# Attention, token mixer and channel mixer in one kernel: float64 weights unpacked without a sign pass, early hidden rows stored as float32, and a new order of all operations

## The chip, the cores and the metric

One core of one Trainium2 chip. The metric is the device time of one execution in microseconds; of several runs the median counts. Times inside an execution come from one profiled execution. Engines are named as in the profile: PE (matmul; PEld is its weight load), DVE (vector), ACT (scalar), POOL (GpSimd), SP (the queue that issues most DMAs).

## The reference, cut to what matters

```python
scores = np.matmul(q, k.T) / 8, masked above the diagonal     # 4 batches x 12 heads, 448 tokens, 64 wide
attn   = exp(scores - max) / (sum + 1e-9);  x = attn @ v      # x: 4 x 448 x 768
u  = x + (relu(x.T @ w_tok1) @ w_tok2).T                      # 448 -> 256 -> 448
y  = u + relu(u @ w_ch1) @ w_ch2                              # 768 -> 1536 -> 768
x_prev = y one token earlier (zeros first)
xk = mu_k*y + (1-mu_k)*x_prev;  xr = mu_r*y + (1-mu_r)*x_prev
out = sigmoid(xr @ w_r) * (relu(xk @ w_k)**2 @ w_v)           # 768 -> 1024 -> 768
```

The weights (w_tok1 to w_r) arrive as float64, q, k and v as float32. The output is float32.

## The kernel before, in words

The matmuls run on two-part numbers: each float32 operand is a rounded high part (ACT makes it by a copy) and the remainder, a low part (DVE subtracts). `mm3` issues three matmuls for each product: high x high, high x low, low x high.

A float64 weight is unpacked in halves of up to 384 columns by `split64` (weights of the token mixer, of w_ch1, w_ch2, w_r) or `load64` (w_k, w_v): SP loads the raw words into `raw`, ACT scales the upper words into `tmp` (`magnitude`), DVE clamps and shifts `tmp` (`shift`), merges the lower words (`assemble`), ACT writes the high part (`high`), DVE or POOL the low part (`low`). In stage 0 `magnitude` takes the absolute value, and a second pass of `assemble` (L307) puts the sign bit back. In stage 1 (`fold`) the sign travels through a Prelu with two slopes, and the second pass is not there.

Stage 0 (`schedule(0)`) holds, for each of the 24 pairs of heads: transposes of k and q (tiles `pt`, `kt`, `qt`), scores (`ps`), row maxima on DVE (`ms`, `nm`, L1396), exponentials on ACT (`e`, L1412), a reciprocal on DVE (`rc`, L1423 and L1426), the multiplication by it (`norm`, L1430, eight for each pair, on POOL or DVE), transposes of `e` on PE (`pe`, L1453), their copies (`et`, L238), the product with v (`pv`) and its transpose (`pn`). The six pairs of batch 0 are scored in float32 (L1375), the others in two parts (L1384). Every three pairs the token mixer follows (`ph`, `pu`, `tok_half`). `early_ch1` fills PE with part of the channel mixer: for batches 0 to 2 it computes 8 of the 12 blocks of relu(u @ w_ch1) (tile `pd`), makes their high and low parts (`relu_hi` L1696, `relu_lo` L1700, tile `he`), and stores both to DRAM (`h_d`). Its 144 groups of three matmuls are the only work in stage 0 that PE can do without a softmax in front of it, from the end of batch 0 on.

Stage 1 (`channel_mixing`, `schedule(1)`) runs batch 3, then 0, 1, 2 through the rest of the channel mixer (tiles `ph`, `acc`), then the gate (`pr`), the products with w_k (`pk`) and with w_v (`pv<-wv`). Where a block was computed early, `h_load` brings both parts back from `h_d` (tile `a`), after the ch2 step four back has begun (`seen[-4]`).

Every operation is registered by `op` with a due time, an engine (or two to choose from), a cost in us, and what it reads, writes and holds. `walk` plays the operations against each other: of those that could start next on an engine it takes the one with the lowest rank (the due time, shifted for some operations by `nudge` with the seeds `NUDGES`, in stage 0 alone), and where two engines are allowed, the one that ends sooner by the costs. The result is the program order of each engine, which the chip then follows; it also decides which `norm`, `low` and copies go to POOL, DVE or ACT.

Of the kernel before, what the change touches and what calls it, by code (L numbers as in the profile page):

```python
# [20 lines left out]
def kernel(  # L21
# [64 lines left out]
    h_d = dpool.tile([B - 1, 8, 128, 2, S], F32, name="h_d")  # L86
# [8 lines left out]
    LAT = {PE: 0.24, ACT: 0.2, DVE: 0.16, POOL: 0.12, SP: 2.6, NONE: 0.0}  # L95
# [3 lines left out]
    class Step:  # L99
        __slots__ = ("t", "eng", "cost", "f", "r", "w", "u", "mode", "phase", "left", "pre", "next", "alt")  # L100
# [4 lines left out]
    state = {"phase": 0, "mode": "F", "dma": 0.0}  # L105

    def op(t, eng, cost, f, *args, r=(), w=(), u=(), mode="F", alt=None):
        x = Step()
        x.t, x.eng, x.cost, x.mode, x.phase = t, eng, cost, mode, state["phase"]
        x.f, x.alt = (f, args), {eng: cost, **(alt or {})}  # L110
        x.r, x.w, x.u = list(r), list(w), list(u)
        steps.append(x)
        for k in x.w:
            makers.setdefault(k, []).append(x)
        for k in x.u:
            users.setdefault(k, []).append(x)

    def walk(mine, rank):
# [35 lines left out]
        while len(out) < len(mine):  # L154
# [31 lines left out]
            free[eng] = s + cost  # L186
            end = s + cost + LAT[eng]
# [18 lines left out]
    NUDGES = tuple(1000000 + n for n in (  # L206
# [5 lines left out]
    ))  # L212
# [31 lines left out]
    LO_BITS = float(np.uint32(896 + 128 << 20).view(np.float32))  # L244
    HI_BITS = float(np.uint32((1151 + 128 << 20) - 1).view(np.float32))
# [6 lines left out]
    def split64(t, key, use, dest, src, pp, n, blocks=False, lead=0):  # L252
# [5 lines left out]
        box, fold = {}, state["phase"] == 1  # L258
# [9 lines left out]
        def magnitude():  # L268
            tmp = wraw.tile([128, 384], F32, tag="tmp", name="tmp")
            box["tmp"] = tmp[:pp, :n]  # L270
            if fold:
                nc.scalar.activation(
                    box["tmp"], box["raw"][:, :, 1].bitcast(F32), AF.Prelu, scale=TINY, alpha=FOLD
                )
                return
            nc.scalar.activation(
                box["tmp"], box["raw"][:, :, 1].bitcast(F32), AF.Abs, scale=65536.0
            )

        def shift():  # L280
            tmp = box["tmp"]
            bits = tmp.bitcast(I32)
            if fold:
                nc.vector.tensor_scalar(
                    out=tmp, in0=tmp, scalar1=NEG_BITS, scalar2=POS_BITS, op0=ALU.max, op1=ALU.min
                )
                nc.vector.tensor_scalar(
                    out=bits, in0=bits, scalar1=3, scalar2=None, op0=ALU.logical_shift_left
                )
                return  # L290
            nc.vector.tensor_scalar(
                out=tmp, in0=tmp, scalar1=LO_BITS, scalar2=HI_BITS, op0=ALU.max, op1=ALU.min
            )
            nc.vector.tensor_scalar(
                out=bits, in0=bits, scalar1=4, scalar2=1,
                op0=ALU.logical_shift_left, op1=ALU.logical_shift_right,
            )

        def assemble():
            raw = box["raw"]  # L300
            bits = box["tmp"].bitcast(I32)
            nc.vector.scalar_tensor_tensor(
                bits, raw[:, :, 0], 29, bits, op0=ALU.logical_shift_right, op1=ALU.bitwise_or
            )
            if fold:
                return
            nc.vector.scalar_tensor_tensor(  # L307
# [1480 lines left out]
```

## Time and profile before

| what | value |
|---|---|
| median of 3 runs | 917.48 us (917.46 to 920.13) |
| the profiled execution's own time | 917.56 us |
| its span, first to last instruction | 915.8 us |
| mean granted TensorE clock | 0.997 |
| PE busy | 899.3 us (98%) |
| DVE, ACT, POOL busy | 650.3, 500.8, 76.0 us |

The span is what the trace covers; the 1.8 us between it and the time of the same execution lie around it. A matmul's record is longer than the time until the next can start, so a busy PE in these views may still have lost some of its time. Stage 0 ends, as far as PE shows it, at about 354 us.

### The profile page before, as it was taken

To read this page: it belongs to the slowest core of one execution; us is meant where nothing else is said; L and a number is where in the kernel's file an instruction comes from. 1 tells how busy PE (TensorE), PEld (TensorE's weight loads), DVE (VectorE), ACT (ScalarE), POOL (GpSimd) and SP (SyncE) were. 2 spreads that over 40 slices of the span, in tenths; PEclk is the share of its full clock that TensorE was granted. 3 is DMA by queue.
4 is the path that set the end of the run, shared out by engine and by line. 5 is a ranking of instruction groups with operands and counts; after the bars stand their busy time and mean duration, and the time that the engine had idled before them with its cause. 6 is when DMAs were issued, how large, how long until landed. Compare 5 with 4: busy or idle time off the path is not lost.

```text
span 915.8 us, 15743 instructions
## 1 busy us (share of the span) xinstructions
PE 899.3 (98%) x5340; PEld 804.4 (88%) x5340; DVE 650.3 (71%) x1547; ACT 500.8 (55%) x1186; POOL 76.0 (8%) x169
## 2 busy tenths in 40 slices
PE   7899999999999999999999999999999999999997
PEld 4577887888888889999999999999999999999997
DVE  6999899985576655777774646559644676789873
ACT  6987777775566654445442324236634566763330
POOL 3332122210110010000000000000000000000000
PEclk9999999999999999999999999999999999999999
DMA  9644666463444212558595895867874264576552
GB/s 199 152 138 105 176 198 175 121 199 99 110 124 130 73 65 83 163 155 296 168 330 207 281 331 201 275 221 239 275 227 138 97 219 128 174 260 185 177 151 61
DMA packets 174128, 162.66 MB, mean 178 GB/s; under 512 B 87584, under 2 KB 160800, under 8 KB 174048
## 3 DMA queue, kind: packets, MB, share of 16 engines
q1 hardware_dynamic: 173120, 161.43, 57.6%
q8 instruction: 42, 0.69, 0.3%
q10 hardware_dynamic: 928, 0.23, 0.1%
q14 instruction: 38, 0.31, 0.1%
HBM read 108.66 MB, written 51.38 MB: 175 GB/s over the span
## 4 chain that ended last, share of the span: by engine, by line
PE 95%; ACT 1%; DVE 1%; POOL 1%; DMA 0%; issue 0%; SPq 0%; POOLq 0%; ACTq 0%
PE acc L554 6%; PE acc L552 6%; PE acc L553 6%; PE pe L1453 5%; PE pv L1469 5%; PE ph L552 4%; PE ph L553 4%; PE ph L554 4%; PE ps L1384 4%; PE pk L552 4%; PE pk L554 4%; PE pk L553 4%; PE pv L553 4%; PE pv L554 4%; PE pv L552 4%; PE pd L552 3%
## 5 line engine op out<-in xcount | busy, mean ns | idle before, releaser
L1412 ACT ACTIVATE e<-ms,nm 112x448 f32<-112x448 f32 (+3 forms) x192 | 100.6, 532 | 17.1 <-DVE nm L1396 16.3
L553 PE MATMUL acc<-a,w 128*128 128x448 f32 x288 | 105.2, 365 | 0.0
L552 PE MATMUL acc<-a,w 128*128 128x448 f32 x288 | 105.2, 365 | 0.0
L554 PE MATMUL acc<-a,w 128*128 128x448 f32 x288 | 105.2, 365 | 0.0
L1396 DVE CUSTOM_DVE_ANT_0 ms<-ps,mask 112x448 f32<-112x448 f32 (+3 forms) x192 | 77.8, 442 | 18.7 <-PE ps L1384 12.2
L238 ACT COPY et<-pe 112x448 f32<-112x448 f32 x109 | 53.5, 539 | 35.5 <-PE pe L1453 35.3
L1430 POOL TENSOR_SCALAR e<-e,rc 112x224 f32<-112x224 f32 (+3 forms) x94 | 52.6, 576 | 211.3 <-DVE rc L1426 133.2
L1453 PE MATMUL pe<-ident,e 112*112 112x112 f32 x480 | 61.8, 267 | 4.9 <-POOL e L1430 2.5
L552 PE MATMUL pv<-wv,kk 128*128 128x384 f32 x196 | 65.5, 334 | 0.0
L554 PE MATMUL pv<-wv,kk 128*128 128x384 f32 x196 | 65.5, 334 | 0.0
L553 PE MATMUL pv<-wv,kk 128*128 128x384 f32 x196 | 65.5, 334 | 0.0
L1453 PEld LDWEIGHTS pe<-ident,e 112*112 112x112 f32 x480 | 50.9, 136 | 14.6 <-POOL e L1430 5.3
L553 PE MATMUL pk<-a,wk 128*128 128x448 f32 x168 | 61.9, 368 | 0.0
L554 PE MATMUL pk<-a,wk 128*128 128x448 f32 x168 | 61.8, 368 | 0.0
L552 PE MATMUL pk<-a,wk 128*128 128x448 f32 x168 | 61.8, 368 | 0.0
L552 PE MATMUL pd<-a,w 128*128 128x448 f32 x144 | 58.1, 403 | 0.0
L552 PEld LDWEIGHTS acc<-a,w 128*128 128x128 f32 x288 | 54.1, 188 | 4.3
L553 PEld LDWEIGHTS acc<-a,w 128*128 128x128 f32 x288 | 54.1, 188 | 4.2
L554 PEld LDWEIGHTS acc<-a,w 128*128 128x128 f32 x288 | 54.1, 188 | 4.2
L418 ACT CAST kk<-a 128x512 fp32r<-128x512 f32 x49 | 30.2, 621 | 49.6 <-PE pv L554 36.5
L554 PE MATMUL pr<-w,a 128*128 128x384 f32 x168 | 56.1, 334 | 0.0
L553 PE MATMUL pr<-w,a 128*128 128x384 f32 x168 | 56.1, 334 | 0.0
(142 smaller groups left out, 2243.2 us busy)
## 6 DMA issues: line engine op xcount, KB each, us to landing
raw<-in_moe_w_ch_dram SPq DMA_DIRECT2D x48, 384.0 KB, 3.7
h_d<-he SPq DMA_DIRECT2D x24, 448.0 KB, 2.9
a<-h_d SPq DMA_DIRECT2D x24, 448.0 KB, 5.4
x_d<-t SPq DMA_DIRECT2D x48, 224.0 KB, 3.5
a<-x_d SPq DMA_DIRECT2D x48, 224.0 KB, 4.4
a<-u_d SPq DMA_DIRECT2D x36, 224.0 KB, 4.1
raw<-in_moe_w_v_dram SPq DMA_DIRECT2D x16, 384.0 KB, 5.5
raw<-in_moe_w_k_dram SPq DMA_DIRECT2D x16, 384.0 KB, 4.1
```

What stands on the lines that cost most here:

```text
L238: nc.scalar.copy(o, i) if by == ACT else nc.vector.tensor_copy(o, i)
L418: nc.scalar.copy(dest()[0], src())
L552: nc.tensor.matmul(o, lh, rh, start=start and i == 0, stop=False, skip_group_check=skip)
L553: nc.tensor.matmul(o, lh, rl, start=False, stop=False, skip_group_check=skip)
L554: nc.tensor.matmul(o, ll, rh, start=False, stop=stop and i == n - 1, skip_group_check=skip)
L1384: nc.tensor.matmul(T["s", j, c], T["q"][r, x, qc], T["k"][r, y, :n], start=i == 0, stop=i == 2,)
L1396: nc.vector.tensor_tensor_reduce(out=ms[:, :n], in0=T["s", j, c], in1=mask[:, S - n:], scale=-0.125, scalar=BIG, op0=ALU.add, op1=ALU.min, ...
L1412: nc.scalar.activation(T["e", j][:, eoff[c]:eoff[c + 1]], T["ms", j, c][:, :n], AF.Exp, bias=T["nm"][:, j, c:c + 1], scale=-1.0, accum_out ...
L1430: (nc.gpsimd if by == POOL else nc.vector).tensor_scalar(out=ec, in0=ec, scalar1=T["rc"][:, j, c:c + 1], scalar2=1.0, op0=ALU.mult, op1=AL ...
L1453: nc.tensor.transpose(pe[:CP, o + (c - kc) * CP:o + (c - kc + 1) * CP], T["e", j][:, eoff[c] + kc * CP:eoff[c] + (kc + 1) * CP], ident[:CP ...
L1469: nc.tensor.matmul(T["pv"][64 * j:64 * j + 64, kc * CP:S], T["vn"][:, kc, j, :], T["et"][:, o:o + S - kc * CP], start=kc == 0, stop=kc == 2,)
```

## The change

1. `split64` always uses the Prelu form: the sign pass of stage 0 (28 instructions on DVE, L307) is gone. `shift` is split into two operations, `clamp` and `shift`, in `split64` and `load64`, so that other operations may come between them.
2. `early_ch1` no longer makes two parts: one Relu on ACT writes float32 rows (4 buffers in place of 2), and `h_d` holds half the bytes. In stage 1 each of the 24 blocks is loaded as float32 and then rounded on ACT (`h_hi`) and subtracted on DVE (`h_lo`).
3. The planner: other costs, an own delay between operations of one engine that depend on each other (`SELF`), and a resource `port` that operations marked `sb` hold one at a time; other due times (`PAIR`, `EV`, the early weights); other seeds. All engines get a new order.

```diff
-    h_d = dpool.tile([B - 1, 8, 128, 2, S], F32, name="h_d")
+    h_d = dpool.tile([B - 1, 8, 128, S], F32, name="h_d")
...
+    SELF = {PE: 0.0, ACT: 0.12, DVE: 0.11, POOL: 0.1, SP: 0.0, NONE: 0.0}
...
-                s = max(s, here if e == eng != SP else end)
+                s = max(s, here + SELF[e] if e == eng != SP else end)
+            if x.sb:
+                s = max(s, state["port"])
...
-    NUDGES = tuple(1000000 + n for n in (
+    NUDGES = (
...
             nc.scalar.activation(
-                box["tmp"], box["raw"][:, :, 1].bitcast(F32), AF.Abs, scale=65536.0
+                box["tmp"], box["raw"][:, :, 1].bitcast(F32), AF.Prelu, scale=TINY, alpha=FOLD
+            )
...
-            if fold:
-                return
-            nc.vector.scalar_tensor_tensor(
-                bits, raw[:, :, 1], -(2 ** 31), bits, op0=ALU.bitwise_and, op1=ALU.bitwise_or
...
-        op(t, DVE, 0.1 + (0.66 + slow) * g, shift, r=[("mag", k)], w=[("bit", k)], u=u[1:])
+        op(t, DVE, 0.09 + 0.19 * g, clamp, r=[("mag", k)], w=[("clp", k)], u=u[1:], sb=True)
+        op(t, DVE, 0.09 + 0.19 * g, shift, r=[("clp", k)], w=[("bit", k)], u=u[1:], sb=True)
...
-        nc.sync.dma_start(h3s[b, j].bitcast(F32), h_d[b, j])
+        nc.sync.dma_start(raw(h3s[b, j]), h_d[b, j])
+
+    def h_hi(b, j):
+        part_hi(h3s[b, j])
+
+    def h_lo(b, j):
+        part_lo(h3s[b, j])
...
+                op(t - 2.2 * BEAT, ACT, 0.46, h_hi, b, j, r=[("hr", b, j)], w=[("hhi", b, j)], u=[a2])
+                op(t - 2.2 * BEAT, DVE, 0.54, h_lo, b, j, r=[("hhi", b, j)], w=[("hh", b, j)], u=[a2], sb=True)
...
-    PAIR = (11.0, 13.0, 15.0, 16.0)
+    PAIR = (10.0, 13.5, 14.5, 14.5)
...
                     op(
-                        s0 + 9.1 + 2 * j + 0.1 * i, POOL, (0.43, 0.53, 0.6, 0.7)[c], norm, j, c,
-                        r=[("rc", g)], w=[("no", j, c, g)], u=[("e", j, g), ("st", g)],
-                        alt={DVE: (0.24, 0.31, 0.42, 0.55)[c]},
+                        s0 + 9.1 + 2 * j + 0.1 * i, POOL, (0.34, 0.43, 0.52, 0.615)[c], norm, j, c,
+                        r=[("rc", g)], w=[("no", j, c, g)], u=[("e", j, g), ("st", g)], sb=True,
+                        alt={DVE: (0.19, 0.245, 0.31, 0.37)[c]},
...
-            def relu_lo(j):
-                t = G["h", j]
-                nc.vector.scalar_tensor_tensor(
-                    t[:, 1], G["p", j][:, :S], 0.0, t[:, 0].bitcast(F32), op0=ALU.max, op1=ALU.subtract
-                )
...
-            ch_weight(n, 60 + 14.0 * n, 7, f"w{n}")
+            ch_weight(n, 70 + 16.0 * n, 8, f"w{n}")
```

What the planner makes of it, counted over the built programs: of the 192 `norm` multiplications 98 stood on DVE and 94 on POOL, now 134 and 58. Of the 28 `low` passes of the early weights 18 stood on POOL, now 10. Of the 120 copies of `pe` to `et` 11 stood on DVE, now 16, the rest on ACT. PE does the same matmuls; it changes 108 times between whole-array matmuls and those that use half of the rows (`ps`) or of the columns (`pv<-et`), now 102 times.

Three places in the order follow. First, the start of the program on DVE, before (tmp and raw are a float64 half of a token-mixer weight on its way, ms and nm the row maxima of pair 0):

```order
L291 TENSOR_SCALAR tmp<-tmp 112x256
L294 TENSOR_SCALAR tmp<-tmp 112x256
L302 SCALAR_TENSOR_TENSOR tmp<-raw,tmp 112x256
L307 SCALAR_TENSOR_TENSOR tmp<-raw,tmp 112x256
L1396 ISA ms,nm<-ps,mask 112x448
```

and now (w_127 is the token-mixer weight, its low part written here):

```order
L282 TENSOR_SCALAR tmp<-tmp 112x256
L289 TENSOR_SCALAR tmp<-tmp 112x256
L295 SCALAR_TENSOR_TENSOR tmp<-raw,tmp 112x256
L282 TENSOR_SCALAR tmp<-tmp 112x256
L289 TENSOR_SCALAR tmp<-tmp 112x256
L295 SCALAR_TENSOR_TENSOR tmp<-raw,tmp 112x256
L304 TENSOR_TENSOR w_127<-tmp,w_127 112x256
L1394 ISA ms,nm<-ps,mask 112x112
```

Two halves and a low part now stand ahead of the first row maximum, where one half stood.

Second, POOL in pairs 0 and 1 (e is the exponentials, rc the reciprocal; the rows behind the second pass on w_127 are those of pair 1), before:

```order
L316 TENSOR_TENSOR w_127<-tmp,w_127 112x256 x2
L1430 TENSOR_SCALAR e<-e,rc 112x112
L1430 TENSOR_SCALAR e<-e,rc 112x448 x2
L1430 TENSOR_SCALAR e<-e,rc 112x224
L1430 TENSOR_SCALAR e<-e,rc 112x112
L1430 TENSOR_SCALAR e<-e,rc 112x336
```

and now:

```order
L304 TENSOR_TENSOR w_127<-tmp,w_127 112x256
L1428 TENSOR_SCALAR e<-e,rc 112x112 x2
L1428 TENSOR_SCALAR e<-e,rc 112x336
L1428 TENSOR_SCALAR e<-e,rc 112x224
L1428 TENSOR_SCALAR e<-e,rc 112x448 x3
```

One weight pass instead of two stands in front of the multiplications of pair 1. In both orders POOL has six of that pair's eight (the last of the three 448-wide ones now belongs to pair 2, which has six on POOL too, where it had four).

Third, DVE in stage 1 while batch 0 goes through the mixer, now, with buffer numbers (a_5843 is an early block that came back from DRAM, ph a block of this stage, w and tmp a weight of the gate):

```order
L295 SCALAR_TENSOR_TENSOR tmp_5882<-raw_5816,tmp_5882 128x384
L627 SCALAR_TENSOR_TENSOR a_5904<-ph_5867,a_5904 128x448
L304 TENSOR_TENSOR w_5911<-tmp_5882,w_5911 128x384
L599 TENSOR_TENSOR a_5843<-a_5843 128x448
L282 TENSOR_SCALAR tmp_5931<-tmp_5931 128x384
```

and at the like place before:

```order
L410 TENSOR_TENSOR tmp_5874<-tmp_5969,tmp_5874 128x384
L637 SCALAR_TENSOR_TENSOR a_5988<-ph_5955,a_5988 128x448
L284 TENSOR_SCALAR tmp_5997<-tmp_5997 128x384
L287 TENSOR_SCALAR tmp_5997<-tmp_5997 128x384
L302 SCALAR_TENSOR_TENSOR tmp_5997<-raw_5939,tmp_5997 128x384
```

The subtraction for the early block is new on DVE; it stands behind a subtraction that needs PE (`a_5904<-ph_5867`), and between the end of that block on PE and the first matmul on a_5843 PE has 73 other matmuls to do. Over the 24 early blocks this distance is 55 to 181 matmuls.

## Rows read from the trace of the kernel before

**Rows 1.** The page: busy time of the engines; chain that ended last.
```profile
PE 899.3 (98%) x5340; PEld 804.4 (88%) x5340; DVE 650.3 (71%) x1547; ACT 500.8 (55%) x1186; POOL 76.0 (8%) x169
...
PE 95%; ACT 1%; DVE 1%; POOL 1%; DMA 0%; issue 0%; SPq 0%; POOLq 0%; ACTq 0%
```

**Rows 2.** Windows by stage: busy us and (x instructions), PEclk, DMA share, GB/s.
```profile
0.00:100.00 100.00, 88.56 (x625) 64.09 (x627) 85.05 (x275) 79.11 (x234) 30.00 (x55) 0.98 0.63 150
100.00:355.00 255.00, 254.96 (x1830) 213.60 (x1827) 187.32 (x543) 171.17 (x472) 41.01 (x73) 1.00 0.45 130
355.00:617.00 262.00, 262.00 (x1295) 242.92 (x1294) 170.28 (x357) 101.72 (x196) 4.25 (x36) 1.00 0.70 234
...
809.00:916.00 107.00, 101.78 (x588) 101.46 (x586) 78.82 (x135) 31.77 (x55) 0.00 (x0) 0.99 0.51 153
```

**Rows 3.** Waits of PE: total us, times, longest.
```profile
PE pt L1350 <- DMA kn<-in_k_dram: 4.1, 1, 4.1
PE pe L1453 <- POOL e L1430: 2.5, 4, 1.7
PE ps L1375 <- ACT qt L1354: 1.3, 2, 0.7
PE pe L1453 <- DVE e L1430: 1.1, 1, 1.1
```

**Rows 4.** Windows of 2 us around the fall of the clock.
```profile
28.00:30.00 2.00, 1.24 (x9) 1.24 (x10) 1.97 (x6) 0.53 (x1) 1.89 (x4) 0.78 0.12 47
30.00:32.00 2.00, 2.00 (x13) 1.89 (x11) 1.90 (x7) 1.95 (x6) 0.41 (x1) 0.50 0.01 2
32.00:34.00 2.00, 2.00 (x16) 1.39 (x16) 1.93 (x6) 2.00 (x6) 0.25 (x1) 0.86 0.69 195
```

**Rows 5.** Timeline of PE: start us, us, what [idle before].
```profile
27.40 0.31 PE L1453 MATMUL pe<-ident,e 112*112 112x112 f32 x1 [1.71 <-POOL e L1430]
28.76 3.49 PE L1453 MATMUL pe<-ident,e 112*112 112x112 f32 x19 [1.05 <-DVE e L1430]
...
40.27 2.43 PE L1453 MATMUL pe<-ident,e 112*112 112x112 f32 x20 [0.57 <-DVE xh L1496]
```

**Rows 6.** Timeline of PE in stage 1, two matmuls in a row.
```profile
503.60 0.36 PE L553 MATMUL ph<-a,w 128*128 128x448 f32 x1
503.80 0.36 PE L554 MATMUL ph<-a,w 128*128 128x448 f32 x1
```

**Rows 7.** Groups of DVE by form, 0 to 355 us: busy us, mean ns.
```profile
L1700 DVE SCALAR_TENSOR_TENSOR he<-pd,he 128x448 fp32r<-128x448 f32 x24 | 14.9, 620 | 15.6 <-ACT he L1696 15.3
...
L1430 DVE TENSOR_SCALAR e<-e,rc 112x448 f32<-112x448 f32 x21 | 12.7, 603 | 0.4
...
L307 DVE SCALAR_TENSOR_TENSOR tmp<-raw,tmp 128x384 int32<-128x384 int32 x20 | 11.2, 558 | 0.7
...
L1430 DVE TENSOR_SCALAR e<-e,rc 112x112 f32<-112x112 f32 x24 | 9.7, 406 | 0.5
```

**Rows 8.** Timeline of DVE: one multiplication by itself.
```profile
322.49 0.45 DVE L1430 TENSOR_SCALAR e<-e,rc 112x448 f32<-112x448 f32 x1
```

**Rows 9.** Groups of POOL by form, 0 to 355 us.
```profile
L1430 POOL TENSOR_SCALAR e<-e,rc 112x448 f32<-112x448 f32 x27 | 19.0, 705 | 59.1 <-DVE rc L1426 32.9 <-ACT xh L1492 18.3 <-ACT h L1600 7.9
...
L316 POOL TENSOR_TENSOR w<-tmp,w 128x384 fp32r<-128x384 f32 x12 | 12.5, 1040 | 29.8 <-ACT w L312 25.0 <-PE pt L1350 4.7
```

**Rows 10.** Timeline: the first row maximum on DVE.
```profile
8.97 0.62 DVE L1396 CUSTOM_DVE_ANT_0 ms<-ps,mask 112x448 f32<-112x448 f32 x1 [0.90 <-PE ps L1375]
```

**Rows 11.** Groups of DVE and ACT by form, 355 to 916 us.
```profile
L609 DVE TENSOR_TENSOR a<-a 128x448 fp32r<-128x448 f32 x42 | 24.4, 619 | 3.7 <-ACT a L606 3.6
...
L606 ACT CAST a<-a 128x448 fp32r<-128x448 f32 x42 | 22.6, 566 | 5.7 <-DMA a<-x_d 3.3 <-DMA a<-u_d 2.1
```

**Rows 12.** The page: DMA issues, KB each, us to landing.
```profile
a<-h_d SPq DMA_DIRECT2D x24, 448.0 KB, 5.4
...
a<-x_d SPq DMA_DIRECT2D x48, 224.0 KB, 4.4
```

More of the change, by code (lines that the diff above doesn't have):

```diff
@@ L94 @@
     PE, ACT, DVE, POOL, SP, NONE = "PE", "ACT", "DVE", "POOL", "SP", "-"
-    LAT = {PE: 0.24, ACT: 0.2, DVE: 0.16, POOL: 0.12, SP: 2.6, NONE: 0.0}
+    LAT = {PE: 0.24, ACT: 0.2, DVE: 0.16, POOL: 0.15, SP: 2.6, NONE: 0.0}
+    SELF = {PE: 0.0, ACT: 0.12, DVE: 0.11, POOL: 0.1, SP: 0.0, NONE: 0.0}
     MODE, STICK, WAIT = 0.1, 1.5, 0.08
@@ L99 @@
     class Step:
-        __slots__ = ("t", "eng", "cost", "f", "r", "w", "u", "mode", "phase", "left", "pre", "next", "alt")
+        __slots__ = ("t", "eng", "cost", "f", "r", "w", "u", "mode", "phase", "left", "pre", "next", "alt", "sb")
     steps, makers, users = [], {}, {}
@@ L104, with op @@
     free = {e: 0.0 for e in (PE, ACT, DVE, POOL, SP, NONE)}
-    state = {"phase": 0, "mode": "F", "dma": 0.0}
-    def op(t, eng, cost, f, *args, r=(), w=(), u=(), mode="F", alt=None):
+    state = {"phase": 0, "mode": "F", "dma": 0.0, "port": 0.0}
+    def op(t, eng, cost, f, *args, r=(), w=(), u=(), mode="F", alt=None, sb=False):
         x = Step()
+        x.sb = sb
         x.t, x.eng, x.cost, x.mode, x.phase = t, eng, cost, mode, state["phase"]
@@ L186, in walk @@
             free[eng] = s + cost
+            if x.sb:
+                state["port"] = s + cost
             end = s + cost + LAT[eng]
@@ L252, in split64 @@
     def split64(t, key, use, dest, src, pp, n, blocks=False, lead=0):
[L258 removed]
+        box = {}
         def load():
@@ L397, in load64 @@
         op(
-            t, ACT, 0.18 + 0.37 * g, magnitude, r=[("raw", k)] + ([last[1]] if last else []),
+            t, ACT, 0.04 + 0.41 * g, magnitude, r=[("raw", k)] + ([last[1]] if last else []),
             w=[("mag", k)], u=u,
         )
-        op(t, DVE, 0.1 + 0.66 * g, shift, r=[("mag", k)], w=[("bit", k)], u=u[1:])
-        op(t, DVE, 0.05 + 0.5 * g, assemble, r=[("bit", k)], w=[key], u=u)
+        op(t, DVE, 0.09 + 0.19 * g, clamp, r=[("mag", k)], w=[("clp", k)], u=u[1:], sb=True)
+        op(t, DVE, 0.09 + 0.19 * g, shift, r=[("clp", k)], w=[("bit", k)], u=u[1:], sb=True)
+        op(t, DVE, 0.05 + 0.43 * g, assemble, r=[("bit", k)], w=[key], u=u, sb=True)
         return (lambda: box["tmp"]), u[1]
@@ L410, in f @@
             (eng.tensor_add if plus else eng.tensor_sub)(o(), x(), y())
-        op(t, DVE, 0.06 + 0.5 * g, f, r=r, w=[key], u=use)
+        op(t, DVE, 0.05 + 0.42 * g, f, r=r, w=[key], u=use, sb=True)
     def split32(t, key, r, use, dest, src, g=1.0):
@@ L422, in low @@
             (nc.gpsimd if by == POOL else nc.vector).tensor_sub(lo, src(), hi.bitcast(F32))
-        op(t, ACT, 0.18 + 0.33 * g, high, r=r, w=[key + ("hi",)], u=use)
+        op(t, ACT, 0.04 + 0.37 * g, high, r=r, w=[key + ("hi",)], u=use)
         op(
-            t, DVE, 0.06 + 0.5 * g, low, r=[key + ("hi",)], w=[key], u=use,
+            t, DVE, 0.05 + 0.42 * g, low, r=[key + ("hi",)], w=[key], u=use, sb=True,
         )
@@ L1119, in total @@
                     def total(name, o, where, x, r, u):
-                        op(te, DVE, 0.63, k_sum, n, q, o, where, x, r=end + [(r, n, q)], w=[(name, n, q)], u=u)
+                        op(te, DVE, 0.54, k_sum, n, q, o, where, x, r=end + [(r, n, q)], w=[(name, n, q)], u=u)
                     if f == "11":
-                        op(te, ACT, 0.54, k_copy, n, q, r=end, w=[("kvx", n, q)], u=[kb["a"], zx])
+                        op(te, ACT, 0.44, k_copy, n, q, r=end, w=[("kvx", n, q)], u=[kb["a"], zx])
                     elif f == "s2":
@@ L1126, in channel_mixing @@
                     elif f == "12":
-                        op(te, ACT, 0.54, k_relu, n, q, r=end, w=[("kr", n, q)], u=[kb["a"], zr])
+                        op(te, ACT, 0.44, k_relu, n, q, r=end, w=[("kr", n, q)], u=[kb["a"], zr])
                     elif f == "s3":
```

144 lines of the change are left out of this document (62 added, 82 removed), and 11 rows, old and new, of the table NUDGES.

## The prediction

> **What bounds the kernel now.** I read the page first. PE is busy for 899.3 of 915.8 us, and PE makes up 95% of the chain that ended last [rows 1]: whatever the change takes off DVE, ACT, POOL or the DMA queues counts only where PE waits for it. The windows by stage show where that can be [rows 2]. From 100 to 355 us PE is busy for 254.96 of 255 us, from 355 to 617 us for 262 of 262; only the first 100 us (88.56 busy) and the end (809 to 916 us, 101.78 busy) have holes. The end is the last evacuation and store behind the last matmul, which the change leaves alone. So 11.4 us of idle PE in the first 100 us are what there is to win, less what can't go away: 4.1 us before the first k has landed [rows 3]. That leaves 7.3 us.
>
> Two things stand behind this idle time and are lost with it. A matmul's record (0.36 us) is longer than the time to the next start (0.20 us) [rows 6], so each wait hides some 0.16 us inside a busy record; for the seven waits of rows 3 behind the first, that is 1.1 us. And the clock: behind the pause that ends with POOL's and DVE's multiplications of pair 1 (1.71 and 1.05 us idle [rows 5]) the granted clock is 0.78, 0.50 and 0.86 in three windows of 2 us [rows 4], so it stood at the lower of its two levels, 1.2 GHz, for a stretch; the missing shares are (0.22 + 0.50 + 0.14) x 2 = 1.7 us. In rows 5 it can be seen: 19 transposes take 3.49 us there, 20 of them 2.43 us at 40.27. The pot in the early part is thus 7.3 + 1.1 + 1.7 = 10.1 us.
>
> **The change part by part.** I sum against the profiled execution's own time, 917.56 us (915.8 of span and 1.8 around it); the median of the runs, 917.48, is the same within 0.1 us.
>
> *Sign pass.* 20 instructions of 0.558 us [rows 7] and 8 narrower ones go: 11.2 to 15.6 us of DVE, I take 14. *Second part of the early blocks.* 24 x 0.620 = 14.9 us of DVE go [rows 7]. Both leave DVE, which is not the bound; they lie beside PE work.
>
> *What the new order puts on DVE in return.* 36 multiplications, between 0.406 us (112 wide) and 0.603 us (448 wide) as they run now [rows 7], about 18 us; 5 copies of et, 448 wide and from PSUM as L1700 is, so some 0.62 us each, 3 us; 8 low parts at no more than the 0.558 of a like pass, up to 4.5 us. That is 25.5 us back for 29 us removed: DVE ends 3.5 us lighter, not 29. It may be more: a 448-wide multiplication that ran by itself took 0.45 us [rows 8], against the mean of 0.603. With 94 such operations on POOL now and 58 after, more of the 134 on DVE run by themselves; at 0.15 us each this is up to 20 us. POOL loses 36 multiplications (at most 0.705 us each) and 8 low parts (at most 1.04 us) [rows 9], up to 33.7 of its 76 us.
>
> The Trainium skill bears on that ("SBUF — State Buffer", section "Who interferes with whom"): a DVE operation of this kind and a GpSimd operation hold a shared port pair in turn, and the later one blocks for the whole instruction of the other. The trace agrees in kind, with 0.45 against a mean of 0.603 us. Taken literally it speaks against the move: if each moved multiplication had to sit out one 448-wide one on POOL, the 36 would cost up to 36 x (0.45 + 0.705) = 41.6 us of DVE, and DVE would end 20 us heavier. By the mean row it ends lighter.
>
> *What PE gets of it, term by term.* (a) The waits for the multiplications, 2.5 + 1.1 = 3.6 us [rows 3], with five of the hidden tails (0.8) and the clock (1.7): 6.1 us. The order speaks for a part only: pairs 3 and on have most multiplications on DVE, but pairs 1 and 2 have six of eight on POOL, behind one weight pass rather than two, and their last one on DVE stands behind row maxima of the next pair. I take half, -3.0; the bounds are 0 and -6.1. (b) The other idle time in the first 100 us, 7.3 - 3.6 = 3.7 us: 1.3 of it waits for ACT's copies of qt [rows 3], which the change doesn't touch, the rest is spread over single waits for copies and parts, which meet shorter queues where the early weights are unpacked later (from 70 in place of 60, every 16 in place of 14). I take a third, -1.2; bounds 0 and -3.7. (c) At the start DVE now has three passes of a second weight half and a low part ahead of the first row maximum, at most 4 x 0.558 = 2.2 us. DVE stood idle for 0.90 us just there, waiting for the scores [rows 10]; what is left, up to 1.3 us, delays pair 0, while PE goes on with the transposes of pairs 1 and 2. I take +0.3. (d) Six changes of the array's mode fewer: taken as 0, at most one hidden tail each, -1.0. (e) From 100 to 355 us: 0, PE has no idle time to give there, and this is what hides the removed passes.
>
> *Early blocks through DRAM as float32.* New in stage 1: 24 x (0.566 + 0.619) us on ACT and DVE [rows 11], 13.6 and 14.9 us, in the stretch from 355 to 617 us. Their cover: ACT is busy for 101.7 and DVE for 170.3 of 262 us there [rows 2], and each load is released four ch2 steps ahead of its use, 4 x 18 matmuls x 0.20 = 14.4 us. Of these the load takes some 4.4 us (the 224 KB rows of x_d, against 5.4 for the present 448 KB [rows 12]), the two passes 1.2 us: 8.8 us stay for standing in the queues of ACT and DVE. The order gives 55 to 181 matmuls, at least 11 us, between the nearest work of PE that the new subtraction stands behind and its use. I take 0; if the cover is gone, what is late is the ch2 step itself, and behind it all of PE. Halved traffic brings nothing either, since no matmul of this stage waits now.
>
> Sum: 917.6 - 3.0 - 1.2 + 0.3 = 913.7 us.
>
> **The rivals.** *More than the pot.* The views of idle time may understate the early loss: PE retires 625 matmuls in the first 100 us and 1830 in the 255 behind them [rows 2], 6.25 against 7.18 per us. If the first 100 us ran at the later rate, they would take 87 us, and the kernel 904.5 us. For it: DVE (85) and ACT (79) are both near full there, so PE is led by the softmax of pairs 0 to 7, and DVE gets relief. Against it: the mix of shapes differs, the 4.1 us at the start stay, and ACT's work hardly shrinks.
>
> *No change.* The multiplications that PE waited for on POOL are waited for on DVE, behind row maxima; pair 1 still pauses, the clock still falls, and (c) eats the rest: 917.6 - 1.2 + 0.3 or so, 916.7 us. For it: two of the first three pairs keep six on POOL.
>
> *Slower, by the new rounding passes.* ch2 needs an early block, whose subtraction stands on DVE behind weight halves and behind a subtraction that waits for PE. It decides once the two queues hold a block for more than the 8.8 us left over; each block that is then late by 0.3 us costs 0.3 us of PE, 24 of them 7.2 us: 924.8 us, or 921 with the gain of the early part. For it: on blocks with a distance of 73 matmuls up to eleven instructions, of 0.56 to 0.62 us at most, stand in between on DVE, some 6 us of the 8.8, and raw loads share SP's queue. Against it: today's loads of twice the size end no wait of PE.
>
> The clock could widen the middle case in either direction: a new pause like that of rows 5 costs its length and 1.7 us. The Trainium skill tells the same of a kernel that idles and falls back to the low clock ("TensorE: Matmul & The Clock Gate", section "HAM oscillation — how this bites in real kernels"); rows 4 are this kernel's instance.
>
> **How the numbers follow.** What three runs of this kernel can tell from no change is about 0.3%, 2.8 us. Gain of part of the pot, 910 to 914.7 us: 0.36, the likeliest, its own range 910 to 914.7. Gain at or beyond the pot, 902 to 910: 0.20. Within 0.3% (914.7 to 920.3): 0.26. Slower by the rounding passes or by new early pauses: 0.18. That makes faster 0.56, same 0.26, slower 0.18. The range leaves out the best few hundredths below 904 and about one in eight above 921.5, where the rounding passes would cost more than the early part brings.
>
> **What would show it.** Right: in the first 100 us PE's idle time falls from 11.4 to some 7 us, the wait of pe for e on POOL shrinks below 1.5 us, the end of stage 0 comes 3 to 5 us sooner than 354 us, and from there on every stage is as long as before, with no wait of acc for a tile a. DVE's mean for a multiplication falls from 0.603 (448 wide) towards 0.45 us. Wrong: idle PE between 355 and 617 us; a low clock at a new place; stage 0 sooner by more than 10 us, which would say that the lost time lay inside busy records; or a stage 0 of the old length.

## The result, and the profile after

| | before | after |
|---|---|---|
| median | 917.48 us (917.46 to 920.13, 4 runs) | 906.59 us (906.09 to 907.14, 4 runs) |
| span of the profiled execution | 915.8 us | 904.1 us |
| mean granted clock | 0.997 | 1.000 |

The ratio is 0.9874, interval 0.9856 to 0.9893: 10.9 us faster, where 3.8 us were forecast. The time is inside the range, near its lower end. The two profiled executions lie 11.5 us apart (917.56 and 906.09); the traces below are theirs.

The page of the kernel after, busy time of the engines:

```profile
PE 892.8 (99%) x5340; PEld 802.9 (89%) x5340; DVE 628.4 (70%) x1568; ACT 507.7 (56%) x1205; POOL 47.8 (5%) x125
```

PE does as many matmuls as before in 6.5 us less of recorded time [rows 1]: part of what was saved had been counted as busy. The windows by stage, after (columns as in [rows 2]):

```profile
0.00:100.00 100.00, 93.62 (x692) 68.79 (x693) 86.97 (x308) 87.67 (x260) 22.84 (x43) 1.00 0.70 167
100.00:355.00 255.00, 255.00 (x1819) 218.13 (x1817) 163.36 (x523) 163.52 (x450) 19.92 (x41) 1.00 0.37 105
355.00:617.00 262.00, 262.00 (x1304) 243.67 (x1304) 188.56 (x397) 120.67 (x235) 4.56 (x36) 1.00 0.69 220
```

The same cut where PE's stages end, before and then after (stage 0; stage 1 up to the first `pr`):

```profile
0.00:354.44 354.44, 342.96 (x2449) 277.16 (x2450) 271.87 (x816) 250.08 (x704) 71.01 (x128) 1.00 0.50 135
354.44:617.09 262.65, 262.65 (x1297) 243.53 (x1296) 170.87 (x358) 102.02 (x198) 4.25 (x36) 1.00 0.70 234
...
0.00:342.86 342.86, 336.48 (x2448) 275.66 (x2449) 243.08 (x814) 245.88 (x698) 42.76 (x84) 1.00 0.47 124
342.86:605.52 262.66, 262.66 (x1298) 243.45 (x1296) 184.90 (x391) 117.12 (x230) 4.56 (x36) 1.00 0.67 216
```

In the first 100 us PE starts 692 matmuls and not 625, its idle time falls from 11.44 to 6.38 us, and DVE is as full as before (86.97 against 85.05): the passes that went made room for others. The waits of PE, over the whole kernel after:

```profile
PE pt L1348 <- DMA kn<-in_k_dram: 4.0, 1, 4.0
PE ps L1373 <- ACT qt L1352: 0.9, 2, 0.7
PE pe L1451 <- ACT qt L1352: 0.5, 1, 0.5
PE ps L1373 <- ACT kt L1352: 0.3, 1, 0.3
PE pe L1451 <- DVE et L246: 0.3, 1, 0.3
PE ps L1373 <- DVE nm L1394: 0.2, 1, 0.2
```

Both waits for `e` of [rows 3], 3.6 us, are gone. With them went the fall of the clock: where [rows 4] have 0.78, 0.50 and 0.86, the same windows after read

```profile
28.00:30.00 2.00, 2.00 (x15) 1.53 (x17) 2.00 (x8) 2.00 (x8) 0.00 (x0) 1.00 0.46 141
30.00:32.00 2.00, 2.00 (x16) 1.11 (x14) 1.97 (x11) 2.00 (x8) 0.13 (x1) 1.00 0.90 277
32.00:34.00 2.00, 1.98 (x19) 1.14 (x16) 2.00 (x13) 2.00 (x8) 2.00 (x4) 1.00 0.17 52
```

How far the kernel after leads on PE. Since the order differs, the first four marks are points at which PE has issued the same matmuls in both kernels, counted by kind from the timelines (us from the span's start):

| mark | before | after | lead |
|---|---|---|---|
| 56 matmuls, before the transposes of `e` of pair 0 | 17.25 | 16.42 | 0.8 |
| 176 matmuls, behind those of pair 1 | 37.56 | 32.68 | 4.9 |
| 605 matmuls, 9 of them for early blocks | 97.44 | 89.13 | 8.3 |
| 1356 matmuls | 199.35 | 188.93 | 10.4 |
| first `ph` of stage 1, 2448 matmuls | 354.44 | 342.86 | 11.6 |
| first `pr` (stage 1's mixer done) | 617.09 | 605.52 | 11.6 |
| end of the span | 915.77 | 904.14 | 11.6 |

All of it is won in stage 0: 4.1 us around pair 1, 3.4 more up to the third mark, and 3.3 behind it. Stage 1 takes 262.65 us from `ph` to `pr` before and 262.66 after.

**What happens at pair 1.** PE after, as a timeline:

```profile
21.64 2.11 PE L1467 MATMUL pv<-et,vn 112*64 112x448 f32 x16
23.67 0.64 PE L1373 MATMUL ps<-kt,qt 64*112 64x224 f32 x4
24.24 0.60 PE L1348 MATMUL pt<-ident,qn 112*128 112x112 f32 x4
24.70 0.62 PE L1485 MATMUL pn<-ident,xT 128*112 128x128 f32 x4
25.16 0.55 PE L1348 MATMUL pt<-ident,kn 112*128 112x112 f32 x4
25.63 1.01 PE L1373 MATMUL ps<-kt,qt 64*112 64x448 f32 x4
26.57 2.44 PE L1451 MATMUL pe<-ident,e 112*112 112x112 f32 x20
```

The 20 transposes of pair 1 start without a wait and take 2.44 us, as the later pair of [rows 5] did. The reciprocal that releases their multiplications, on DVE, before and then after, and the six multiplications on POOL after:

```profile
26.24 0.17 DVE L1423 TENSOR_SCALAR rc<-sm 112x8 f32<-112x8 f32 x1
```
```profile
22.98 0.17 DVE L1421 TENSOR_SCALAR rc<-sm 112x8 f32<-112x8 f32 x1
...
23.49 3.01 POOL L1428 TENSOR_SCALAR e<-e,rc 112x112 f32<-112x112 f32 x6 [0.98 <-DVE rc L1424]
```

POOL is no faster and has as many of them. They run 3.3 us sooner, beside five steps of PE for pairs 0, 2, 3 and 4 that stand in front of the transposes; before, PE came to the transposes at 25.70 us with nothing else in front of them, and the reciprocal had not been started.

### The profile page after: what moved, and what is told of

Its sections match the earlier page's. It is cut to its first block, busy times and chain, and to the rows that moved or that the text cites. A ratio compares the mean times of both kernels' runs of the same rounds, so it can differ in the third digit from the quotient of the medians.

```text
span 904.1 us, 15752 instructions
## 1 busy us (share of the span) xinstructions
PE 892.8 (99%) x5340; PEld 802.9 (89%) x5340; DVE 628.4 (70%) x1568; ACT 507.7 (56%) x1205; POOL 47.8 (5%) x125
## 4 chain that ended last, share of the span: by engine, by line
PE 94%; ACT 3%; DVE 1%; DMA 1%; issue 0%; SPq 0%
PE acc L544 6%; PE acc L542 6%; PE acc L543 6%; PE pv L1467 5%; PE pe L1451 4%; PE ph L542 4%; PE ph L544 4%; PE ph L543 4%; PE pk L544 4%; PE pk L543 4%; PE pk L542 4%; PE pv L544 4%; PE pv L543 4%; PE pv L542 4%; PE ps L1382 3%; PE pd L542 3%
## 5 line engine op out<-in xcount | busy, mean ns | idle before, releaser
L1410 ACT ACTIVATE e<-ms,nm 112x336 f32<-112x336 f32 (+3 forms) x192 | 100.5, 530 | 12.5 <-DVE nm L1394 11.7
L599 DVE TENSOR_TENSOR a<-a 128x448 fp32r<-128x448 f32 x84 | 51.0, 627 | 19.1 <-ACT a L596 19.0
L246 ACT COPY et<-pe 112x448 f32<-112x448 f32 x104 | 50.9, 540 | 21.5 <-PE pe L1451 21.4
L596 ACT CAST a<-a 128x448 fp32r<-128x448 f32 x84 | 46.0, 567 | 24.7 <-DMA a<-h_d 20.2
L1451 PE MATMUL pe<-ident,e 112*112 112x112 f32 x480 | 57.6, 261 | 0.9 <-ACT qt L1352 0.5
L543 PE MATMUL pr<-w,a 128*128 128x384 f32 x168 | 56.1, 334 | 0.0
```

Of the source, the lines that this page charges most:

```text
L246: nc.scalar.copy(o, i) if by == ACT else nc.vector.tensor_copy(o, i)
L543: nc.tensor.matmul(o, lh, rl, start=False, stop=False, skip_group_check=skip)
L596: nc.scalar.copy(t[:, 0], raw(t))
L599: nc.vector.tensor_sub(t[:, 1], raw(t), t[:, 0].bitcast(F32))
L1410: nc.scalar.activation(T["e", j][:, eoff[c]:eoff[c + 1]], T["ms", j, c][:, :n], AF.Exp, bias=T["nm"][:, j, c:c + 1], scale=-1.0, accum_out ...
L1451: nc.tensor.transpose(pe[:CP, o + (c - kc) * CP:o + (c - kc + 1) * CP], T["e", j][:, eoff[c] + kc * CP:eoff[c] + (kc + 1) * CP], ident[:CP ...
```

## The experiments

Three questions: does the lighter work or the order bring the gain, do the places of the multiplications matter, and what in the order does it. The kernel before, run beside them, took 917.5 to 918.0 us (medians); ratios are to it.

### Lighter work and order, one without the other

`new_heavy`: the order of the kernel after with the 28 sign passes and the 24 passes over the early blocks put back, each right behind the pass that feeds it; the second kind writes a tile that nothing reads.

```diff
+            if first:
+                nc.vector.scalar_tensor_tensor(
+                    bits, box["raw"][:, :, 1], -(2 ** 31), bits, op0=ALU.bitwise_and, op1=ALU.bitwise_or
...
+                t = ud.tile([128, S], F32, tag="hx", name="hx", bufs=2)
+                nc.vector.scalar_tensor_tensor(t, G["p", j][:, :S], 0.0, G["h", j], op0=ALU.max, op1=ALU.subtract)
```

> The changed kernel in its own order, with the removed DVE passes put back: the 28 sign passes, and 24 passes that read pd behind the Relu and write an unused tile. If the lighter DVE brought the gain, most of the 10.9 us is lost again, 914 to 918 us. If the new order brought it, the passes go beside PE work and the time stays within 3 us of 906.6.

922.34 us, ratio 1.0052 (1.0037 to 1.0067). `old_light`: the order of the kernel before without both kinds of passes; the early blocks lack their low part (the high part stands in DRAM twice, so that loads and bytes stay).

```diff
-            nc.vector.scalar_tensor_tensor(
-                bits, raw[:, :, 1], -(2 ** 31), bits, op0=ALU.bitwise_and, op1=ALU.bitwise_or
-            )
...
-                nc.sync.dma_start(h_d[b, j], G["h", j].bitcast(F32))
+                nc.sync.dma_start(h_d[b, j], G["h", j].bitcast(F32).unsqueeze(1).to_broadcast([128, 2, S]))
```

> The kernel before in its own order, without the 28 sign passes (Prelu in place of Abs) and without the 24 passes for the low part of the early blocks; both halves of a row in DRAM hold the high part, so the low part of these blocks is left out. If the lighter DVE brought the gain, 906 to 910 us. If the order did, 915 to 918 us.

916.52 us, ratio 0.9987 (0.9978 to 0.9997). So the four corners are 917.5 (old order, old work), 916.5 (old, light), 922.3 (new, old work) and 906.6 (new, light): lighter work alone gives about 1 us, the new order alone costs 5, together they give 11. `new_heavy` is slower than either of its two theories allowed. (Each order was planned for its own work and tuned by its own list of nudges, so the corners show how an order fits its work, and not what an order is worth by itself; `new_heavy` also keeps the new rounding passes of stage 1.) In the old order the relief doesn't reach PE: it still waits 2.0 us for POOL's and 1.8 for DVE's multiplications. In the new order with the old work PE is starved far beyond the early part; windows of `new_heavy` (PE busy first):

```profile
100.00:150.00 50.00, 46.75 (x332) 38.35 (x331) 48.23 (x141) 37.78 (x100) 3.69 (x5) 1.00 0.60 168
150.00:200.00 50.00, 47.70 (x349) 39.41 (x349) 35.52 (x111) 32.96 (x93) 5.71 (x10) 1.00 0.48 132
```

Next, which of the two reliefs, each put back alone in the new order (`new_sign`, `new_low`: one of the two pieces of the diff above).

> The changed kernel with its order, and the 28 sign passes alone put back on DVE (20 of them some 0.56 us), not the 24 passes over the early blocks. Both together cost 15.8 us. Theory of DVE's load (what counts is how much DVE has to do in stage 0): the sign passes are half of the added time, so 913 to 916. Theory of the one bank (the passes over the early blocks cost nearly all, since pd has a single bank that comes free only behind its second reader): 907 to 909.5. Theory of the first pairs (it is the weights unpacked in the first 60 us that hold up the softmax): 917 or more, with a wait of pe for e and a granted clock below 1 between 20 and 40 us.

> The changed kernel with its order, and only the 24 DVE passes that read pd behind ACT's Relu put back (their result goes into a tile that nothing reads). DVE's load: 913 to 916. One bank: 918 to 922, with waits of pd for DVE's hx and the first pd where the changed kernel has it (63.6 us). First pairs: 909 to 911, since these passes stand behind 64 us.

913.87 us (0.9957, 0.9944 to 0.9971) and 912.71 us (0.9942, 0.9930 to 0.9954): 7.3 us for 28 passes (14.9 us of DVE in `new_sign`: 20 of 0.559, 4 of 0.528 and 4 of 0.392), 6.1 us for 24 (15.0 us in `new_low`, 0.624 each). Each costs 0.4 to 0.5 us for each us of DVE, and together they cost 15.8, more than the sum of 13.4. The load counts, not its place; neither the one bank of `pd` nor the first pairs carry it alone. The 912.71 lies just below what the load theory allowed.

### POOL or DVE for the multiplications

`new_pool`: kernel after, the first 36 multiplications that stood on DVE go to POOL at the same places, 98 and 94 as before. `old_light_dve`: `old_light` with the first 36 moved the other way (early blocks as there).

```diff
+                if by == DVE and len(flipped) < 36:
+                    flipped.append(1)
+                    by = POOL
```

> The changed kernel in its own order, the first 36 multiplications that stand on DVE given back to POOL at the same places, so that 98 and 94 are divided as before. If the early waits for POOL were what the move took away, the time goes up by 5 us or more and the wait of pe for e on POOL is back among the longest. If the division doesn't matter, it stays within 2 us of 906.6.

> The order of before without the 28 sign passes and the 24 passes for the low part (left out as in old_light), and with the first 36 of POOL's multiplications on DVE at the same places. If the lighter DVE and the move together make the gain, without any new order, 907 to 911 us. If the order is needed, 914 to 918 us, near the 916.5 of old_light.

908.47 us (0.9895, 0.9880 to 0.9910), only 1.9 more than the kernel after, and 922.23 us (1.0042, 1.0028 to 1.0056), 5.7 more than `old_light` and slower than either theory allowed. In `new_pool` the wait for POOL is back, but it is short, of the size of the whole loss, and the clock stays at 1.00:

```profile
PE pe L1455 <- POOL e L1432: 1.9, 3, 0.9
```

In `old_light_dve` the multiplications stand on DVE behind weight passes and row maxima: PE waits 5.8 us for them in 11 waits, and the clock is at 0.74 between 20 and 40 us. So the division between the two engines, on which my term (a) rested, is worth 1.9 us in the new order and is not what most of the gain is made of.

### The planner: rules, due times, seeds

`old_noseed` and `new_noseed` plan without the list of nudges; `new_noself` also without the own delay and the shared `port`, `new_olddue` with the old due times; `new_seed_a` and `new_seed_b` have one arbitrary nudge in place of the list.

```diff
-        for seed in NUDGES if phase == 0 else ():
+        for seed in ():
```

> The kernel before planned without its 76 seeds, the base for the run before it. If seeds matter little, within 3 us of 917.5. If the old seeds were worth as much as the new ones, both kernels lose alike, some 5 to 15 us each, and the distance between them stays near 11 us.

> The changed kernel planned without any of the 86 seeds. If the planner's new costs, due times and the lighter work carry the gain, it stays below 912 us. If the gain sits in the chosen seeds, it goes back to 915 us or more.

> The changed kernel planned without seeds, and without the two new rules of the planner (own delay, shared port); 106 multiplications fall on DVE and 86 on POOL. If the two rules made the unseeded gain (935.4 to 924.7), it goes back to 932 us or more. If the lighter work, the costs and the due times made it, it stays at 921 to 928 us.

> The changed kernel planned without seeds, and with the due times of before (PAIR, EV, early weights from 60 every 14). If the later early weights and the new due times made the unseeded gain, 932 us or more. If not, 921 to 928 us.

> The changed kernel planned by its own rules with one arbitrary nudge in place of the list. Without nudges it took 924.7, with the list 906.6. If orders by the same rules lie within 2 us of each other: 922.7 to 926.7. If a small shift of a few steps moves the time by many microseconds: outside of it, anywhere from 915 to 932.

> As the other nudged plan, with another arbitrary nudge that shifts a larger share of the steps (2% of them, by up to 3 us). Within 2 us of the plan without nudges: 922.7 to 926.7; a wide spread: outside of it.

| kernel | us | ratio |
|---|---|---|
| `old_noseed` | 935.38 | 1.0195 (1.0174 to 1.0215) |
| `new_noseed` | 924.71 | 1.0077 (1.0057 to 1.0097) |
| `new_noself` | 929.20 | 1.0131 (1.0107 to 1.0154) |
| `new_olddue` | 920.07 | 1.0028 (1.0012 to 1.0044) |
| `new_seed_a` | 928.90 | 1.0120 (1.0103 to 1.0137) |
| `new_seed_b` | 918.89 | 1.0006 (0.9995 to 1.0016) |

The lists are worth 17.9 us in the old kernel and 18.1 in the new one, and without them the distance is 10.7 us. It would be easy to read from this that the rules make the gain. They may not: two nudged plans by the same rules lie 10 us apart, on both sides of the plan without nudges. A single unlisted plan says little about its rules, and the differences of `new_noself` (+4.5) and `new_olddue` (-4.6) are of the size of that spread. `new_noself` fell between the ranges of its two theories, `new_olddue` just below both.

### The place at pair 1

Five kernels in which only the order of a few instructions changes. `new_pair1`: in the kernel after, DVE takes pair 1's reciprocal and one multiplication behind five more row maxima of pair 2. `new_pe1`: in the kernel after, PE alone changes; four transposes of pair 1 stand ahead of the five steps that were in front of them (20 matmuls by the traces, not 18 as expected below).

```diff
+        if phase == 0:      # new_pe1
+            first = [130, 131, 132, 133, 135, 136, 138, 144, 155]
+            out[129:156] = [out[n] for n in first + [n for n in range(129, 156) if n not in first]]
...
+            late = [123, 126, 128, 132, 135, 138, 144, 149, 152]      # new_pair1
+            rest = [n for n in range(123, 153) if n not in late]
+            k = rest.index(145) + 1
+            out[123:153] = [out[n] for n in rest[:k] + late + rest[k:]]
```

> The changed kernel with three DVE steps moved, nothing added or removed: pair 1's reciprocal and one of its multiplications stand behind five more row maxima of pair 2, so that the reciprocal comes 2 to 2.5 us later, at some 25.3 us; all other queues keep their order. Theory of the pause: PE waits 1.5 to 2.5 us for e of pair 1 at 26.6 us, the clock falls behind it, and the kernel takes 2 to 4.5 us longer, 908.5 to 911. Theory of the whole order: the wait is made up behind pair 1, 906 to 907.5.

> The changed kernel with one edit of PE's order alone: the first four transposes of e of pair 1 stand ahead of 18 matmuls (the last scores of pair 2, three turned tiles q, xT and k, the first scores of pair 3) and no longer behind them. Their multiplications end on POOL at about 25.9 us, as before. Theory of PE's order (what PE has in front of the transposes decides whether it stands): PE waits some 2 us for e from 23.7 us on, ACT and DVE get the next scores as much later, and the time is 908.5 to 911. Theory of the queues of ACT and DVE (PE's order matters little, since the softmax sets the pace): the wait is made up again at the next one, 906 to 907.5.

909.48 us (0.9909, 0.9895 to 0.9922) and 910.67 us (0.9917, 0.9903 to 0.9930): 2.9 and 4.1 us lost by one edit each, and not made up later: the first `pr` comes at 608.50 and 610.62 us, 3.0 and 5.1 later than after (the profiled execution of `new_pe1` took 0.5 us more than its median, that of the kernel after 0.5 less). In `new_pair1` PE idles for 2.0 us at the transposes with PE's order as it was, so the time of the reciprocal matters beside PE's order; the fall of the clock that was expected there didn't come. PE in `new_pe1`, the timeline and then three windows:

```profile
24.73 0.28 PE L1454 MATMUL pe<-ident,e 112*112 112x112 f32 x1 [0.42 <-DVE e L1431]
25.39 0.31 PE L1454 MATMUL pe<-ident,e 112*112 112x112 f32 x1 [0.38 <-POOL e L1431]
26.44 0.62 PE L1454 MATMUL pe<-ident,e 112*112 112x112 f32 x2 [0.74 <-POOL e L1431]
26.99 1.09 PE L1376 MATMUL ps<-kt,qt 64*112 64x224 f32 x4
```
```profile
24.00:26.00 2.00, 0.90 (x6) 0.26 (x2) 1.93 (x10) 1.67 (x6) 1.94 (x5) 1.00 0.84 204
26.00:28.00 2.00, 1.56 (x6) 0.72 (x6) 0.00 (x0) 0.00 (x0) 1.00 (x2) 0.60 0.34 76
28.00:30.00 2.00, 2.00 (x13) 1.81 (x12) 0.71 (x3) 0.62 (x2) 0.00 (x0) 0.55 0.00 0
```

This is the pause of [rows 5] made on purpose: 1.54 us of idle PE, then the clock at the lower of its two levels with (0.40 + 0.45) x 2 = 1.7 us lost. DVE and ACT stand still from 26 to 28 us, since the scores that they would work on are behind the transposes. That is 3.2 of the 4.1 us.

Now the reverse, in the kernel before. `old_pair1` takes pair 1's reciprocal and multiplications forward on DVE and puts the pieces of three weight halves, on DVE and ACT, in a row behind pair 1's transposes; `old_pair1b` spreads these pieces among the row maxima of pair 2; `old_light_pair1` is the latter on `old_light` (early blocks as there). PE's order stays.

```diff
+            late = [115, 120, 121, 125, 128, 129, 132, 136, 145, 148, 154, 155, 157, 159, 162]      # old_pair1
+            rest = [n for n in range(115, 165) if n not in late + [127, 131, 138]]
+            k = rest.index(140) + 1
+            out[115:165] = [out[n] for n in rest[:k] + [127, 131, 138] + rest[k:] + late]
```

> The kernel before with one place in its order changed, nothing added or removed: on ACT and DVE the pieces of three weight halves that stand between the exponentials and the reciprocal of pair 1 are put behind the transposes of pair 1; DVE takes the reciprocal and its two multiplications ahead of a row maximum of pair 2 and a low part. PE, POOL and SP keep their order. Theory of the pause (the stall at pair 1 with the clock's fall is a large part of the 10.9 us, and it comes from pair 1's reciprocal at 26.2 us): the reciprocal comes about a microsecond sooner, the granted clock stays above 0.95, and 2 to 4 us are won, 913.5 to 915.5. Theory of the whole order (DVE's and ACT's queue is late everywhere in the first 60 us; moving it at one place moves the wait to pair 2): 916.5 to 918.5, with a new wait behind pair 2.

> The kernel before, with the queues of ACT and DVE changed between the reciprocal of pair 1 and the row maxima of pair 2, nothing added or removed: reciprocal and multiplications of pair 1 first, and the pieces of the three weight halves spread one by one among the row maxima of pair 2, so that no cluster stands ahead of these. PE and POOL keep their order; on SP one load of a raw half goes behind a load of q. Theory of the pause: transposes of pair 1 start at 26.3 us or sooner, the 3.3 us wait for the row maxima that the first try had is gone, and the kernel takes 912.5 to 915.5 us. Theory of the whole order: the queues of ACT and DVE have no slack anywhere before 60 us, a wait of a microsecond or more comes behind pair 2, and the time is 916.5 to 919.

> The same edit of the order on the version of the kernel before with the lighter work (no sign passes, no low parts of the early blocks; the low part of the early blocks is left out of the result). That version took 916.5 us. If relief pays as soon as the pause at pair 1 is gone: 908 to 912.5. If the old order loses at many places, of which pair 1 is one: 914 to 916.

921.62 us (1.0041, 1.0028 to 1.0053), 918.65 (1.0005, 0.9996 to 1.0014) and 917.10 (0.9987, 0.9978 to 0.9997); the first and the last are slower than either of their theories allowed. In `old_pair1` the transposes start at 26.27 us, 1.1 sooner, and the wait moves one pair on:

```profile
38.18 1.47 PE L1380 MATMUL ps<-kt,qt 64*112 64x448 f32 x3 [3.31 <-DVE nm L1401]
```

The scores of pair 3 wait for row maxima of pair 2, which stand behind the weight pieces. In `old_pair1b` that wait is gone and the transposes start at 25.85 us, but POOL's multiplications still come one by one, and the clock stays low for longer than before:

```profile
28.00:30.00 2.00, 1.61 (x8) 1.26 (x9) 1.97 (x8) 1.26 (x4) 0.95 (x2) 0.57 0.16 34
30.00:32.00 2.00, 2.00 (x11) 1.21 (x9) 1.90 (x7) 1.88 (x6) 0.00 (x0) 0.50 0.22 81
32.00:34.00 2.00, 2.00 (x12) 1.65 (x12) 1.30 (x7) 1.73 (x7) 0.66 (x1) 0.50 0.67 192
34.00:36.00 2.00, 2.00 (x14) 0.79 (x14) 1.52 (x8) 0.94 (x3) 0.00 (x0) 0.72 0.71 163
```

That is 3.4 us, against 1.7 in [rows 4]. In `old_light_pair1` the clock doesn't fall at all, and still nothing is won over `old_light` (916.52): the transposes of pair 1 end 2.0 us sooner (29.00 against 30.96), of which 0.4 are left at the first `pd` (71.90 against 72.27). PE still waits 2.0 us for POOL's multiplications, 1.19 of them at pair 1, and other waits stand elsewhere, of 1.1 us (`pn` for `xT`), 1.0 (`pe` for `xh`) and 0.8 (`pv` for `et`).

None of the three edits removes the pause at pair 1, so what the old kernel would gain without it isn't shown. What they show is that moving work on ACT and DVE alone didn't mend it, and that saving the clock there gave nothing in the old order. In the new order both things are shown to matter, what PE has in its own queue in front of the transposes (`new_pe1`) and when the reciprocal comes (`new_pair1`), and a pause made there costs 3 to 4 us for good. The reverse edit, work put in front of the transposes in the old order of PE, was not run.

## Why the prediction was right and wrong

**The bound and the place: right.** PE's early part is where most of the time was; stage 1, with its new rounding passes, kept its length to 0.01 us. DVE and ACT have 14.0 and 15.1 us more to do there than before, near the 14.9 and 13.6 of the forecast, and PE waits for none of it. The early blocks land in 4.2 us and not in 5.4 [rows 12], and nothing waits for them.

The sum was 913.7 us, the profiled execution took 906.09. Of the 7.6 us between them (a) has 3.1 and (e) about 4. These are the two steps that failed.

**Term (a), half of the waits for multiplications and of the clock: should have been all.** It was to bring 3.0 us, with 6.1 as its bound. The bound came: the 3.6 us of waits and the 1.7 of the clock are gone, and with the waits, by my estimate, their hidden tails (0.8 us, which no view shows by itself). I reasoned that pair 1 keeps six multiplications on POOL and so keeps waiting. The count was right and the conclusion wrong: POOL takes 3.01 us for them after as it took 3.07 before, but I looked at who does the work, and not at what PE has in front of it nor at when the reciprocal comes. `new_pool` shows the first (1.9 us), `new_pe1` and `new_pair1` the second (4.1 and 2.9). The order of PE, of which my text gave nothing but the changes of the array's mode, was the one to read at that place.

**Term (b), a third of the other idle time, 1.2 us: right in size.** Of 3.7 us some 2.4 are left (6.38 less the 4.0 of the first k).

**Term (c), +0.3 at the start: too dear.** The first row maximum begins at 8.73 us, where it began at 8.97 [rows 10]; the new passes fit into DVE's idle time in front of it.

**Term (e), nothing from idle-free time: wrong by 4 us.** (a) and (b) as they came, with 0.1 at the first k, make 7.5 us; the lead is 8.3 at the third mark and 11.6 at the end of stage 0. From that mark to the end of stage 0 PE shows 0.04 us of idle time in either kernel, and still the same matmuls take 3.3 us less. I had written that a stage 0 sooner by more than 10 us would say that lost time lay inside busy records, and that is the case: PE's busy time in stage 0 falls by 6.5 us, of which the clock accounts for 1.7. Counted from each start to the next, without idle time, 3.5 of the 6.5 us lie in the transposes of `e` (tile `pe`), 1.0 in those of k and q (`pt`), 0.8 in the scores. A transpose of `e` usually follows the last one after 0.10 us; more than 0.12 us pass in 62 places before and in 24 after, 17 of the 62 and 5 of the 24 at pair 1, where the clock fell before. `new_low` shows the same from the other side: its first `pd` comes 0.6 us later than after (64.17), its idle PE between 100 and 355 us grows by 2.8 us (252.24 busy of 255), and its stage 0 ends 6.7 us later (first `ph` at 349.54): 3.3 us are lost with no idle time to show for it. What holds these matmuls wasn't settled, nor what part term (d) has in it: of the changes of the array's mode 68 stood behind the third mark before and 58 after.

**What the passes' removal is worth: the premise behind (e).** I held that the new order gives DVE nearly all of it back, 25.5 of 29 us, and that what is left hides beside PE work. Neither came. DVE has 28.8 us less to do in stage 0 (271.87 and 243.08), where I had 3.5 and at most 20 more; and the load isn't hidden, since putting it back costs 15.8 us in the new order. In the old order taking it off is worth 1. The relief was a condition of the new order, not a term to be added to it, and a sum of terms can't show that.

**The rival nearest to the result** was "more than the pot" (904.5 us): the first 100 us at the later rate. It fits in part: ACT went from 79.1 to 87.7 us of these 100, and 8.3 us of the lead are there by the third mark. But it put all of its 13 us into the first 100 us, and 3.3 of the 11.6 came later, at the rate it took as given, so that its time is near partly by luck. "Slower by the rounding passes" and "no change" are out.

**Prices.** A multiplication on DVE was to fall from 0.603 towards 0.45 us (448 wide); it did, as a group of DVE in stage 0 shows (busy, mean ns), but not for the reason that I gave, fewer of them on POOL. The last line is `new_pool`, with 94 on POOL as before:

```profile
L1428 DVE TENSOR_SCALAR e<-e,rc 112x448 f32<-112x448 f32 x27 | 12.3, 461 | 0.2
...
L1428 DVE TENSOR_SCALAR e<-e,rc 112x112 f32<-112x112 f32 x34 | 10.0, 312 | 0.2
...
L1432 DVE TENSOR_SCALAR e<-e,rc 112x448 f32<-112x448 f32 x21 | 9.6, 466 | 0.2
```

What changed is when the two engines work. Of the 98 multiplications on DVE 90 overlapped an operation of POOL in time before, 32 of 98 in `new_pool`, 45 of 134 after; their records add up to 50.4, 38.1 and 52.0 us. In the kernel after, the 112-wide ones that met none took 0.27 us (median of 24), those that met one 0.35 (median of 10). So 36 more multiplications cost DVE 1.6 us, where I had 18. (The one of [rows 8] was not by itself either: POOL began one 0.09 us behind it, at 322.58 us.) The rule of the shared `port` in the planner asks for just this: without it and the own delay, in `new_noself`, 96 of 106 overlap, and with both, in `new_noseed`, 40 of 139. The literal reading of the shared port ("SBUF — State Buffer", section "Who interferes with whom", of the Trainium skill), by which DVE would end up 20 us heavier, took each moved multiplication to meet one on POOL; of the 134 that DVE now has, two thirds meet none.

**What stays open.** One edit at pair 1 accounts for 3 to 4 of the 10.9 us, and the marks put 4.1 us of the lead there. The rest is spread over the later pairs, but no run takes it apart, and none changes the overlap of DVE and POOL by itself at an order that is otherwise the same.

## What to carry to other kernels

When a change rewrites an order, read first the row of the engine that bounds, at the place of its longest wait: here what stands in its queue ahead of the waiting instruction, and when the awaited work can begin, mattered more (4.1 and 2.9 us) than which engine does that work (1.9 us). When a plan moves work between two engines, look at whether they run at the same time; here that set the price of the moved work. Compare two orders only where the same work is done. Cut work and new order should be measured crosswise before either gets the credit: here one alone gave 1 us, the other alone lost 5, and both gave 11, and the orders were tuned to their work. Where orders come out of a search, two arbitrary plans by the same rules can lie 10 us apart, so a rule's worth can't be read from a single plan of each kind.

## What was not expected of the hardware

The length of a pause doesn't decide by itself whether the clock falls. In `new_pair1` (rows below) PE idles 1.04 and 0.92 us in two successive rows of 2 us and keeps the full clock, in `new_pe1` (rows above) it idles 1.10 and 0.44 and loses it:

```profile
26.00:28.00 2.00, 0.96 (x5) 0.13 (x1) 1.71 (x5) 2.00 (x9) 1.93 (x3) 1.00 0.94 212
28.00:30.00 2.00, 1.08 (x8) 0.77 (x9) 0.33 (x1) 0.61 (x4) 1.78 (x4) 1.00 0.66 170
30.00:32.00 2.00, 2.00 (x18) 1.68 (x18) 2.00 (x7) 1.43 (x4) 0.00 (x0) 1.00 0.00 0
```

So 1.96 us of idle time cost 2.9 us of the kernel there, and 1.54 us cost 4.1 in `new_pe1`, the difference being of the size of what the clock took (1.7). A fall cost 1.7 us in the kernel before, in `new_pe1` and twice in `old_pair1`, and 3.4 us in `old_pair1b`. Why one set of pauses lowers the clock and the other doesn't, no run here shows.
